# Attention and two feed-forwards on one core: gate and value by seven products of quarter blocks in place of eight

## The chip, the core and the metric

The kernel runs on one core of a Trainium2 chip. The metric is the device time of one execution in microseconds (us), from the first to the last instruction and a little around them. TensorE is called PE here and its loads of stationary operands PEld; VectorE is DVE, ScalarE is ACT, GpSimd is POOL, and SyncE, which issues the transfers, is SP.

## What is computed

Attention over 4 batches of 12 heads (448 tokens, 64 columns each), then a feed-forward with SiLU, then a second one with a gate and a value, all in float32. The part that the change touches is the last one, for 1792 tokens of 768 columns and 1536 hidden columns:

```python
def _moe2_ref(x, w_gate, w_val, w_out):
    g = x @ w_gate
    silu = g * (1.0 / (1.0 + np.exp(-g)))
    val = x @ w_val
    return (silu * val @ w_out).astype(np.float32)
```

## The kernel before

Each float32 matrix is held as two float16 parts, a high and a low one, and each product of matrices is three products of parts: high by high, high by low, low by high, summed in PSUM in float32. So each 128x128 piece of weights costs three matmuls, and each of them has a load of weights of its own.

The program is a list of operations with the engines that may run each, what each reads and writes, and a due time. A planner (`Plan.emit`) goes through the list once, when the program is built, keeps a clock for each engine by formulas for the length of each operation, and hands every operation to an engine and a place in its order; the numbers in `TUNE` (shifts of due times in `FINE`, `OFF`, `WIN`, `WOUT`; the letters A, D, P for the engines allowed; `CUT` for when the weights of the first feed-forward are loaded) steer it. The order on each engine is then fixed, and every queue, SP's too, runs in order: what waits holds up what stands behind it.

The stages overlap: attention of one batch (L706 scores, L816 probabilities by v) runs among the first feed-forward of the batch before it (`ffn1_h` L1011, `ffn1_o` L1051), which writes its result, transposed, to the DRAM tensor `x2d`. `load_gv` and `load_w_out2` bring the weights of the second feed-forward and split them; all of them then stay in SBUF.

The second feed-forward goes over the tokens in blocks of 512, 512, 512 and 256 columns. For a block, `bring_x2` loads x from `x2d` in six pieces of 128 rows, scales and splits them into `XT`. `ffn2_gv` goes over 12 chunks of 128 hidden columns: a chunk takes 6 pieces x 3 matmuls for the gate into one PSUM bank and as many for the value into another (L1206); ACT applies SiLU to the gate (L1211), DVE multiplies by the value out of PSUM (L1213), and ACT, DVE and POOL split the result into the high and the low part (L1216, L1217, L1218 or L1219) in `G`. Then `ffn2_out` takes 128 tokens at a time: two halves of 384 output columns, each 12 x 3 matmuls with the split activations as weights (L1250 to L1252), drained by ACT (L1255) and DVE (L1257) and stored to `out`. The output of one block and the gate and value of the next are interleaved on PE, and only four of the eight PSUM banks serve gate and value.

## Time and profile before

| | before |
|---|---|
| median of 3 runs | 1258.47 us (1258.27 to 1259.04) |
| the profiled execution, its own time | 1259.7 us |
| span of the profiled execution, first to last instruction | 1257.9 us |
| mean granted clock of TensorE over the span, of full speed | 0.98 |
| PE busy | 1178.2 us, 6612 matmuls |
| DVE, ACT, POOL busy | 687.2, 669.4, 492.0 us |
| moved by DMA | 140.61 MB |

The profile is one execution, taken by the hardware profiler. Busy time of an engine is the time in which at least one of its instructions ran; matmuls are pipelined, so several run at a time, and their mean length is longer than the step from one to the next. The granted clock is what TensorE's throttle let through, as a share of full speed. A releaser is whatever ended an idle stretch of an engine. L numbers are lines of the kernel before.

### The profile page before, as it was taken

What the parts mean: (1) busy time and instruction counts of PE and PEld (TensorE: products, weight loads), DVE (VectorE), ACT (ScalarE), POOL (GpSimd) and SP (SyncE); (2) the same over time, 40 slices, a digit from 0 to 9 for tenths busy, and PEclk for the clock granted to TensorE, in tenths of its full rate; (3) what the DMA queues carried; (4) which work ended last, traced back from release to release, by engine and by line L of the source; (5) the groups of instructions that cost most, each with busy time, mean ns of one, the idle gap of its engine ahead of it and who ended that gap; (6) DMA issues with size and microseconds to landing.
All of it is one profiled execution on the core that took longest, in us unless ns stands there. A gap on an engine that the chain in (4) does not pass through costs nothing.

```text
span 1257.9 us, 17505 instructions
## 1 busy us (share of the span) xinstructions
PE 1178.2 (94%) x6612; PEld 599.2 (48%) x6612; DVE 687.2 (55%) x1181; ACT 669.4 (53%) x1219; POOL 492.0 (39%) x474
## 2 busy tenths in 40 slices
PE   5989987799679999999999999999999999999998
PEld 3334443344334444444445454445544555446685
DVE  4788876688756575565459887873111301112121
ACT  4989967677669865898536435652111301112131
POOL 5565456454658897677721624120000100000000
PEclk9999999799889999999999999999999999999999
DMA  7565634479877688567774455502000101000101
GB/s 193 167 155 144 220 131 145 103 174 199 184 149 144 125 191 176 110 126 149 145 238 138 146 173 180 187 1 63 26 14 1 34 26 26 1 1 22 39 1 26
DMA packets 218581, 140.61 MB, mean 112 GB/s; under 512 B 156032, under 2 KB 210816, under 8 KB 218496
## 3 DMA queue, kind: packets, MB, share of 16 engines
q1 hardware_dynamic: 218496, 139.49, 44.3%
q8 instruction: 52, 0.85, 0.3%
q14 instruction: 33, 0.27, 0.1%
HBM read 85.79 MB, written 11.01 MB: 77 GB/s over the span
## 4 chain that ended last, share of the span: by engine, by line
PE 46%; DVE 5%; DMA 2%; POOL 1%; ACT 1%; issue 1%; POOLq 0%; ACTq 0%
PE ps L1206 25%; PE ps L1051 6%; PE ps L1250 4%; PE ps L1252 4%; PE ps L1251 4%; DMA ATT<-in_moe_w_val_dram 1%; DVE W L842 1%; PE ps L816 1%; PE ps L1011 1%; PE ps L706 1%; DVE ATT L890 1%; DVE G L1030 1%; DVE ATT L880 1%; DVE ATT L879 1%; DMA ATT<-ATT 1%
## 5 line engine op out<-in xcount | busy, mean ns | idle before, releaser
L1206 PE MATMUL ps<-XT,W 128*128 128x512 f16 (+1 forms) x1440 | 294.0, 352 | 3.8 <-ACT ER L1211 1.9
L1051 PE MATMUL ps<-G,W 128*128 128x448 f16 x1152 | 240.7, 355 | 4.0 <-DVE G L1041 4.0
L1011 PE MATMUL ps<-XT,W 128*128 128x448 f16 x1152 | 234.9, 353 | 8.2 <-ACT FT L1017 1.7
L1206 PEld LDWEIGHTS <-W 128*128 128x128 f16 x1440 | 141.0, 98 | 131.0 <-issue 5.1
L1011 PEld LDWEIGHTS <-W 128*128 128x128 f16 x1152 | 110.7, 99 | 120.5 <-issue 26.0
L1051 PEld LDWEIGHTS <-W 128*128 128x128 f16 x1152 | 107.9, 98 | 122.3 <-issue 28.9
L1216 ACT ACTIVATE G<-ER 128x512 f16<-128x512 f32 (+1 forms) x48 | 27.6, 575 | 167.3 <-DVE ER L1213 162.2
L1213 DVE SCALAR_TENSOR_TENSOR ER<-ER,ST,ps 128x512 f32<-128x512 f32 (+1 forms) x48 | 32.6, 680 | 151.5 <-PE ps L1206 151.4
L723 ACT ACTIVATE ER<-ps,ST 128x448 f32<-128x448 f32 x144 | 103.1, 719 | 12.1 <-POOL ATT L745 8.8
L1218 POOL TENSOR_SCALAR G<-ER 128x512 f16<-128x512 f32 x20 | 12.6, 629 | 245.5 <-DVE ER L1217 241.2
L715 DVE TENSOR_REDUCE ST<-ps 128x2 f32<-128x896 f32 x96 | 92.4, 966 | 27.8 <-PE ps L706 23.4
L1250 PE MATMUL ps<-W,G 128*128 128x384 f16 x308 | 100.4, 326 | 0.0
L1251 PE MATMUL ps<-W,G 128*128 128x384 f16 x308 | 100.4, 326 | 0.0
L1252 PE MATMUL ps<-W,G 128*128 128x384 f16 x308 | 100.4, 326 | 0.0
L1257 DVE SCALAR_TENSOR_TENSOR ATT<-ps,ST,ATT 128x384 f32<-128x384 f32 x28 | 17.3, 618 | 151.0 <-ACT ATT L1255 151.0
L1255 ACT ACTIVATE ATT<-ps,ST 128x384 f32<-128x384 f32 x28 | 16.2, 580 | 136.7 <-PE ps L1252 136.7
L745 POOL TENSOR_TENSOR ATT<-ER,ATT 128x448 f16<-128x448 f32 x77 | 86.0, 1117 | 6.4
L706 PE MATMUL ps<-ATT 128*64 128x448 f16 x560 | 75.3, 371 | 9.1 <-ACT ER L723 4.0
L1030 DVE SCALAR_TENSOR_TENSOR G<-FT,ST,G 128x448 f16<-128x448 f32 x64 | 57.5, 907 | 20.1 <-ACT G L1022 18.2
L744 POOL TENSOR_SCALAR ER<-ER,ST 128x448 f32<-128x448 f32 x77 | 56.7, 736 | 22.8 <-ACT ATT L739 11.8
L1206 PE MATMUL ps<-XT,ATT 128*128 128x512 f16 (+1 forms) x288 | 60.4, 352 | 0.0
L739 ACT ACTIVATE ATT<-ER,ST 128x448 f16<-128x448 f32 x71 | 45.5, 660 | 20.0 <-DVE ST L731 11.7
(221 smaller groups left out, 1889.4 us busy)
## 6 DMA issues: line engine op xcount, KB each, us to landing
ATT<-in_moe_w_out_dram SPq DMA_DIRECT2D x24, 768.0 KB, 4.3
W<-in_moe_w_in_dram SPq DMA_DIRECT2D x16, 768.0 KB, 6.1
ATT<-in_moe_w_gate_dram SPq DMA_DIRECT2D x12, 768.0 KB, 4.7
ATT<-in_moe_w_val_dram SPq DMA_DIRECT2D x12, 768.0 KB, 5.9
...
ATT<-in_v_dram SPq DMA_DIRECT2D x8, 672.0 KB, 7.2
...
```

The source lines that it names most:

```text
L706: nc.tensor.matmul(out=sp[64 * h:64 * h + 64, u, 0:S], lhsT=T[:, 0, t, 64 * h:64 * h + 64], rhs=T[:, a, :, 64 * h:64 * h + 64], start=(a = ...
L715: op(DVE, 1.04 * S * nt + 65, lambda sp=sp, nm=nm, nt=nt: nc.vector.tensor_reduce(nm, sp[:, 0:nt, 0:S], AX.X, ALU.max, negate=True), r=sk, ...
L723: op(ACT, 705, lambda e=e, u=u, t=t, sp=sp: nc.scalar.activation(e, sp[:, u, 0:S], AF.Exp, bias=st["nb"][:, t:t + 1], scale=eS, accum_out= ...
L744: nc.gpsimd.tensor_scalar(e, e, r1, 1.0, ALU.mult, ALU.mult)
L745: nc.gpsimd.tensor_tensor(lo, e, hi, ALU.subtract)
L1011: nc.tensor.matmul(out=ps[:, 0:S], lhsT=w[:, a, kk], rhs=xt1((b * HP + kk) % NX, x), start=(kk == 0 and s == 0), stop=(kk == KD - 1 and s ...
L1030: DVE: (t_stt(S), lambda gt=gt, hi=hi, lo=lo, s1=s1: nc.vector.scalar_tensor_tensor(lo, gt, s1, hi, ALU.mult, ALU.subtract), True),
L1051: nc.tensor.matmul(out=ps[:, 0:S], lhsT=w[:, a, P * m:P * m + P], rhs=GV1[:, f, x], start=(f == 0 and s == 0), stop=(f == NF1 - 1 and s == 2))
L1206: nc.tensor.matmul(out=ps[:, 0:n], lhsT=w[:, aa, kk], rhs=xt2(kk, x)[:, 0:n], start=(kk == 0 and s == 0), stop=(kk == KD - 1 and s == 2))
L1250: nc.tensor.matmul(out=ps[:, 0, 0:384], lhsT=hi, rhs=wh, start=(f == 0), stop=(f == NF2 - 1))
L1251: nc.tensor.matmul(out=ps[:, 1, 0:384], lhsT=hi, rhs=wlo, start=(f == 0), stop=False)
L1252: nc.tensor.matmul(out=ps[:, 1, 0:384], lhsT=lo, rhs=wh, start=False, stop=(f == NF2 - 1))
```

## The change

Gate and value of a block are a product of x (768 rows, in two halves of 384) with the two weight matrices. The block's tokens are cut into two halves, which makes the product one of a 2x2 arrangement of blocks by another; such a product takes eight products of blocks, and Winograd's form of Strassen's method takes seven, of sums and differences of the blocks.

- **Sums of weights.** `make_sums` makes, for each of the 12 chunks, four sums of quarter blocks of the gate's and the value's weights (ten operations of 384 columns on DVE), splits them (1536 columns: ACT the high part, DVE the low one) and stores them to a new DRAM tensor `s2d`. It is planned during block 0.
- **Sums of x.** `bring_sums` takes the place of `bring_x2` for blocks 1 to 3: three pieces; each loads two halves of x, makes four sums on DVE or POOL, and splits seven quarter blocks at once.
- **Seven products.** `ffn2_seven` takes the place of `ffn2_gv` for blocks 1 to 3: a chunk has seven products of 3 pieces x 3 matmuls, of half the block's columns; five PSUM banks a chunk, out of a ring of all eight; ACT copies the first product out, DVE adds the others to it in SBUF (five adds), and SiLU, the multiply and the split then read SBUF. The sums of weights come from `s2d` in two buffers, one load of 768 KB for each chunk.
- **Blocks** are of 512, 512, 384 and 384 tokens. Two of the four buffers `YS` now hold loaded sums, so the output has two in place of four.
- `FT` and `DG` become parts of one tile `FD`, whose 1024 columns serve as one of two buffers for the adds.
- The tables in `TUNE` are changed throughout: `FINE` (110 entries in place of 86), `OFF`, and many of the letters for engines; so the order of the earlier stages moves too.

```diff
-    PATIENCE={'silu': 2351.866, 'exp': 6600.368},
-    CUT=(0, 1, 1, 7, 10, 13, 16),
+    PATIENCE={'silu': 4305.451, 'exp': 12651.286},
...
+    CUT=(0, 1, 1, 11, 11, 13, 16),
...
-    WIN=83.7,
-    WOUT=99.3,
+    WIN=61.6,
+    WOUT=85.5,
...
+    SU='D',
+    SUH='A',
+    XU='DP',
...
-    FT = pool.tile([P, 2, S], F32, name="FT")
+    FD = pool.tile([P, 2 * S + 2 * P], F32, name="FD")
+    FT = FD[:, 0:2 * S].rearrange("p (a c) -> p a c", a=2)
+    DG = FD[:, 2 * S:].rearrange("p (a c) -> p a c", a=2)
...
+    s2d = dram.tile([NF2 * P, 3072], F16, name="s2d")
...
-    blocks = [(c, min(NB2, NT - c)) for c in range(0, NT, NB2)]
+    blocks = [(0, 512), (512, 512), (1024, 384), (1408, 384)]
+    assert sum(n for _, n in blocks) == NT
+    KH = KD // 2
...
+    T_GW = 82.0
...
+    XU = att32(O_XF, 1792)
+    XW = [XT[:, 3584 * i:3584 * i + 3584] for i in range(2)] + [ER.rearrange("p a c -> p (a c)").bitcast(F16)]
+
+    def bring_sums(i, z, due):
+
+        c0, n = blocks[i]
+        h = n // 2
+        bs = range(c0 // S, (c0 + n - 1) // S + 1)
+        s = s_x2[z][0]
+        if i == 1:
+            marker([], [("xf", r) for r in range(4)] + [("xu", 0, a) for a in range(2)] + [("ft2", r) for r in range(3)] + [(k, kk) for k in ("x2h", "x2l") for kk in range(KD)])
+        for kk in range(KH):
+            x = 0
+            xu, keys = XU[:, 0:7 * h], [("xf", r) for r in range(4)]
+            for a in range(2):
+                row = P * (kk + KH * a)
+                op(SP, t_dma(P * n * 4), lambda xu=xu, a=a, row=row: nc.sync.dma_start(out=xu[:, 5 * h * a:5 * h * a + n], in_=x2d[row:row + P, c0:c0 + n]),
+                   r=[("x2d", b, kk + KH * a) for b in bs] + ["attn_done"], w=[("xu", x, a)], due=due - 12 + kk, late=DMA_LATE)
+            t = xu.rearrange("p (s c) -> p s c", s=7)
+            ab = [("xu", x, 0), ("xu", x, 1)]
+            for d, a, b, alu in ((3, 6, 1, ALU.subtract), (1, 1, 0, ALU.subtract), (2, 3, 0, ALU.add), (4, 5, 2, ALU.subtract)):
+                add(only(TUNE["XU"], {
+                    DVE: (t_tt(h), lambda t=t, d=d, a=a, b=b, alu=alu: nc.vector.tensor_tensor(t[:, d], t[:, a], t[:, b], alu), True),
+                    POOL: (t_ptt(h), lambda t=t, d=d, a=a, b=b, alu=alu: nc.gpsimd.tensor_tensor(t[:, d], t[:, a], t[:, b], alu))}), r=ab, w=keys, due=due + kk)
+            split(XW[kk][:, 0:7 * h], XW[kk][:, 1792:1792 + 7 * h], xu, keys + ab, s, [("sx2", z), ("silu", B - 1)], [("x2h", kk)], [("x2l", kk)], due + kk, 7 * h)
+
+    US, SH = STG[0].bitcast(F32)[:, 0:1536], STG[1].bitcast(F16)[:, 0:3072]
+    SB = [(STG[2].bitcast(F16)[:, 0:3072], [("st2", 2)]), (ATT[:, (O_Y + 2 * CB) // 2:(O_Y + 4 * CB) // 2], [("ys", 2), ("ys", 3)])]
+
+    def make_sums():
+        marker([], ["U0", ("st2", 0)])
+        marker([], ["SHh", "SHl", ("st2", 1)])
+        us = US.rearrange("p (s c) -> p s c", s=4)
+        uk = [("U", s) for s in range(4)]
+        for f in range(NF2):
+            due = t_out2(0) + 6.0 * f
+            (gb, gk), (vb_, vk) = slot2(2 * f), slot2(2 * f + 1)
+            (gh, gl), (vh, vl) = [[t[:, 768 * a:768 * a + 768] for a in range(2)] for t in (gb, vb_)]
+            lo, hi = slice(0, 384), slice(384, 768)
+            for dst, terms in ((0, ((vh[:, lo], vh[:, hi], ALU.add), (vl[:, lo], ALU.add), (vl[:, hi], ALU.add))),
+                               (2, ((gh[:, lo], vh[:, lo], ALU.subtract), (gl[:, lo], ALU.add), (vl[:, lo], ALU.subtract))),
+                               (1, ((us[:, 0], gh[:, lo], ALU.subtract), (gl[:, lo], ALU.subtract))),
+                               (3, ((gh[:, hi], us[:, 1], ALU.subtract), (gl[:, hi], ALU.add)))):
+                for x, t in enumerate(terms):
+                    a, b, alu = t if x == 0 else (us[:, dst], *t)
+                    add(only(TUNE["SU"], {
+                        DVE: (t_tt(384), lambda dst=dst, a=a, b=b, alu=alu: nc.vector.tensor_tensor(us[:, dst], a, b, alu), True),
+                        POOL: (t_ptt(384), lambda dst=dst, a=a, b=b, alu=alu: nc.gpsimd.tensor_tensor(us[:, dst], a, b, alu))}),
+                        r=gk + vk + ["U0"] + [uk[0]] * (dst == 1) + [uk[1]] * (dst == 3), w=[uk[dst]], due=due)
+            sh, sl = SH[:, 0:1536], SH[:, 1536:3072]
+            add(only(TUNE["SUH"], {
+                ACT: (t_act(1536), lambda: nc.scalar.activation(sh, US, AF.Copy)),
+                DVE: (t_ts(1536), lambda: nc.vector.tensor_copy(sh, US), True),
+                POOL: (t_pts(1536), lambda: nc.gpsimd.tensor_scalar(sh, US, 1.0, 1.0, ALU.mult, ALU.mult))}), r=uk, w=["SHh"], due=due)
+            add(only(TUNE["SU"], {
+                DVE: (t_tt(1536), lambda: nc.vector.tensor_tensor(sl, US, sh, ALU.subtract), True),
+                POOL: (t_ptt(1536), lambda: nc.gpsimd.tensor_tensor(sl, US, sh, ALU.subtract))}), r=uk + ["SHh"], w=["SHl"], due=due)
+            op(SP, t_dma(P * 6144), lambda f=f: nc.sync.dma_start(out=s2d[P * f:P * f + P], in_=SH), r=["SHh", "SHl"], w=[("s2d", f)], due=due, late=DMA_LATE)
+
+    Z = [G[:, 12288:14336].bitcast(F32), FD[:, 0:1024]]
+    RING = [(PS_F[i], ("F", i)) for i in range(3)] + [(PS_X, "psx")] + [(PS_S[i][:, u], ("S", i, u)) for i in range(2) for u in range(2)]
...
+    def ffn2_seven(i, z):
+        c0, n = blocks[i]
+        h = n // 2
+        t0 = t_blk2(i)
+        step = 6.8 * n / 512.0
+        for f in range(NF2):
+            u = fn2[0]
+            fn2[0] += 1
+            sb, sbk = SB[u % 2]
+            op(SP, t_dma(P * 6144), lambda sb=sb, f=f: nc.sync.dma_start(out=sb, in_=s2d[P * f:P * f + P]), r=[("s2d", f)], w=sbk, due=t0 + step * (f - 2), late=DMA_LATE)
+            z4 = Z[u % 2]
+            zk = [("z", u % 2, x) for x in range(4)]
+            (g, gk), (v1, vk) = slot2(2 * f), slot2(2 * f + 1)
+            g, v1 = [t.rearrange("p (a k c) -> p a k c", a=2, k=KD) for t in (g, v1)]
+            sw = sb.rearrange("p (a s k c) -> p s a k c", a=2, s=4, k=KH)
+            at = [0]
+
+            def product(bank, o, w, wk, x):
+                ps, pk = bank
+                for kk in range(KH):
+                    def mm(kk=kk):
+                        for s, (aa, xx) in enumerate(((0, 0), (0, 1), (1, 0))):
+                            c = 1792 * xx + h * x
+                            nc.tensor.matmul(out=ps[:, h * o:h * o + h], lhsT=w[:, aa, kk], rhs=XW[kk][:, c:c + h],
+                                             start=(kk == 0 and s == 0), stop=(kk == KH - 1 and s == 2))
+                    op(PE, 3 * (h / 2.4 + 0.5), mm, r=wk + [("x2h", kk), ("x2l", kk)], w=[pk], due=t0 + step * f + 0.3 * at[0])
+                    at[0] += 1
+
+            def take():
+                bn2[0] += 1
+                return RING[bn2[0] % 8]
+
+            def plus(d, nd, bank, o, src, r):
+                ps, pk = bank
+                dst, pp, nn = z4[:, h * d:h * (d + nd)], ps[:, h * o:h * (o + nd)], nd * h
+                if src is None:
+                    sr = z4[:, 3 * h:4 * h].unsqueeze(1).to_broadcast([P, 2, h])
+                    dst, pp = dst.rearrange("p (a c) -> p a c", a=2), pp.rearrange("p (a c) -> p a c", a=2)
+                else:
+                    sr = z4[:, h * src:h * (src + nd)]
+                op(DVE, t_tt(nn), lambda: nc.vector.tensor_tensor(dst, pp, sr, ALU.add), r=[pk] + r, w=zk[d:d + nd], due=-1e4)
+            b1, b6, b2, b57, b34 = take(), take(), take(), take(), take()
+            product(b1, 0, g[:, :, 0:KH], gk, 0)
+            op(ACT, t_act(h, True), lambda z4=z4, ps=b1[0]: nc.scalar.activation(z4[:, 0:h], ps[:, 0:h], AF.Copy), r=[b1[1]], w=zk[0:1], due=-1e4)
+            product(b6, 0, sw[:, 1], sbk, 2)
+            plus(3, 1, b6, 0, 0, zk[0:1])
+            product(b2, 0, g[:, :, KH:KD], gk, 5)
+            plus(0, 1, b2, 0, 0, zk[0:1])
+            product(b57, 0, sw[:, 0], sbk, 1)
+            product(b57, 1, sw[:, 2], sbk, 3)
+            plus(1, 2, b57, 0, None, zk[3:4])
+            plus(3, 1, b57, 0, 2, zk[2:3])
+            product(b34, 0, sw[:, 3], sbk, 6)
+            product(b34, 1, v1[:, :, KH:KD], vk, 4)
+            plus(1, 2, b34, 0, 1, [])
+            gt, vt = z4[:, 0:n], z4[:, n:2 * n]
+            op(ACT, t_act(n, False, 1), lambda gt=gt, f=f: nc.scalar.activation(gt, gt, AF.Silu, scale=dg[:, f:f + 1]),
+               r=[("dg", f)], w=zk[0:2], due=-1e4, table="silu")
+            op(DVE, t_stt(n), lambda gt=gt, vt=vt, f=f: nc.vector.scalar_tensor_tensor(gt, gt, c2[:, f:f + 1], vt, ALU.mult, ALU.mult),
+               shared=True, r=[("c2", f)], w=zk, due=-1e4)
+            hi, lo = GV2[:, f, 0, 0:n], GV2[:, f, 1, 0:n]
+            op(ACT, t_act(n), lambda gt=gt, hi=hi: nc.scalar.activation(hi, gt, AF.Copy), r=zk[0:2], w=[("Gh", f)], due=-1e4)
+            op(DVE, t_tt(n), lambda gt=gt, hi=hi: nc.vector.tensor_tensor(gt, gt, hi, ALU.subtract), shared=True, r=[("Gh", f)], w=zk[0:2], due=-1e4)
+            add({POOL: (t_pts(n), lambda gt=gt, lo=lo: nc.gpsimd.tensor_scalar(lo, gt, 2.0 ** 11, 1.0, ALU.mult, ALU.mult)),
+                 ACT: (t_act(n), lambda gt=gt, lo=lo: nc.scalar.activation(lo, gt, AF.Copy, scale=2.0 ** 11))},
+                r=zk[0:2], w=[("Gl", f)], due=-1e4)
...
-    OT = YS
+    OT = YS[0:2]
...
-        ffn2_gv(i, zone(i))
+        (ffn2_seven if i else ffn2_gv)(i, zone(i))
+        if i == 0:
+            plan.tag = "sums"
+            make_sums()
+            plan.tag = None
         if i + 1 < len(blocks):
-            bring_x2(i + 1, zone(i + 1), t_blk2(i) + T_GV)
+            bring_sums(i + 1, zone(i + 1), t_out2(i))
```

The orders of DVE and SP around the place, as the program has them. First DVE, before, where the output of block 0 runs among the first chunks of block 1 (L1213 multiply, L1217 subtract, L1257 drain of the output):

```order
992 L1217 TENSOR_TENSOR ER<-ER,G 128x512
993 L1257 SCALAR_TENSOR_TENSOR ATT<-ps,ST,ATT 128x384 x6
994 L1213 SCALAR_TENSOR_TENSOR ER<-ER,ST,ps 128x512
995 L1217 TENSOR_TENSOR ER<-ER,G 128x512
996 L1257 SCALAR_TENSOR_TENSOR ATT<-ps,ST,ATT 128x384 x2
997 L1213 SCALAR_TENSOR_TENSOR ER<-ER,ST,ps 128x512
```

And DVE after the change at the same place (L1282 and L1291 make the sums of weights, L1340 are the adds of products, L1402 the drain of the output):

```order
1083 L1282 TENSOR_TENSOR ATT<-ATT,W 128x384 x6
1084 L1402 SCALAR_TENSOR_TENSOR ATT<-ps,ST,ATT 128x384
1085 L1282 TENSOR_TENSOR ATT<-W,ATT 128x384
1086 L1340 TENSOR_TENSOR G<-ps,G 128x256
1087 L1282 TENSOR_TENSOR ATT<-ATT,W 128x384
1088 L1340 TENSOR_TENSOR G<-ps,G 128x256
1089 L1402 SCALAR_TENSOR_TENSOR ATT<-ps,ST,ATT 128x384
1090 L1291 TENSOR_TENSOR ATT<-ATT 128x1536
1091 L1282 TENSOR_TENSOR ATT<-ATT 128x384
1092 L1340 TENSOR_TENSOR G<-ps,G 128x512
1093 L1282 TENSOR_TENSOR ATT<-ATT 128x384
1094 L1340 TENSOR_TENSOR G<-ps,G 128x256
```

The drains of products now stand in one queue with the sums of weights; row 1090 ends the eighth of twelve sums, and the last one ends at row 1190, among the adds of chunk 8 of block 1.

SP before, from the last weights on (L868 weights, L1186 x, L1261 output):

```order
265 L868 DMA ATT<-in_moe_w_out_dram 128x1536 x8
266 L1186 DMA ATT<-x2d 128x512 x6
267 L1261 DMA out_dram<-ATT 64x768 x8
268 L1186 DMA ATT<-x2d 128x512 x2
269 L1186 DMA ATT<-x2d 128x256 x4
```

And SP after, from the end of block 1's chunks to the start of block 3's x (L1293 stores sums of weights, L1309 loads them, L1252 x, L1406 output):

```order
293 L1293 DMA s2d<-ATT 128x3072
294 L1309 DMA ATT<-s2d 128x3072 x3
295 L1252 DMA ATT<-x2d 128x384 x4
296 L1406 DMA out_dram<-ATT 64x768 x2
297 L1252 DMA ATT<-x2d 128x384 x2
298 L1406 DMA out_dram<-ATT 64x768 x4
299 L1309 DMA ATT<-s2d 128x3072
300 L1406 DMA out_dram<-ATT 64x768 x2
301 L1309 DMA ATT<-s2d 128x3072 x11
302 L1252 DMA ATT<-x2d 128x384 x4
```

Where SP had nothing but x and outputs, each chunk now has a load of sums, which waits until PE is done with the buffer.

## Rows read from the trace of the kernel before

**Rows 1.** The page: busy time by engine, and the chain that ended last.

```profile
PE 1178.2 (94%) x6612; PEld 599.2 (48%) x6612; DVE 687.2 (55%) x1181; ACT 669.4 (53%) x1219; POOL 492.0 (39%) x474
...
PE 46%; DVE 5%; DMA 2%; POOL 1%; ACT 1%; issue 1%; POOLq 0%; ACTq 0%
PE ps L1206 25%; PE ps L1051 6%; PE ps L1250 4%; PE ps L1252 4%; PE ps L1251 4%; DMA ATT<-in_moe_w_val_dram 1%; DVE W L842 1%; PE ps L816 1%; PE ps L1011 1%; PE ps L706 1%; DVE ATT L890 1%; DVE G L1030 1%; DVE ATT L880 1%; DVE ATT L879 1%; DMA ATT<-ATT 1%
```

**Rows 2.** Windows: stretch and length, each engine's busy us, PE clock, DMA.

```profile
50.00:400.00 350.00, 301.99 (x1641) 142.66 (x1640) 268.12 (x488) 270.84 (x509) 196.39 (x173) 0.93 0.65 158
...
840.00:1200.00 360.00, 360.00 (x1965) 192.10 (x1964) 75.47 (x110) 71.27 (x116) 18.62 (x27) 1.00 0.08 22
```

**Rows 3.** Timeline of PE: start, length of the row, line, shape, number of matmuls.

```profile
842.07 10.52 PE L1206 MATMUL ps<-XT,W 128*128 128x512 f16 x48
...
1191.83 2.35 PE L1206 MATMUL ps<-XT,W 128*128 128x256 f16 x20
...
1249.69 0.33 PE L1251 MATMUL ps<-W,G 128*128 128x384 f16 x1
...
1252.29 0.33 PE L1252 MATMUL ps<-W,G 128*128 128x384 f16 x1
```

**Rows 4.** Groups of instructions, PEld: busy us, mean ns of one; idle before.

```profile
L1206 PEld LDWEIGHTS <-W 128*128 128x128 f16 x1440 | 141.0, 98 | 131.0 <-issue 5.1
```

**Rows 5.** Timeline of PEld: start, length of the row, number of loads.

```profile
122.53 0.11 PEld L1011 LDWEIGHTS <-W 128*128 128x128 f16 x2 [0.36 <-issue]
...
1191.94 2.06 PEld L1206 LDWEIGHTS <-W 128*128 128x128 f16 x19
```

**Rows 6.** Groups of instructions, DVE, by shape.

```profile
L1217 DVE TENSOR_TENSOR ER<-ER,G 128x512 f32<-128x512 f32 x36 | 27.7, 770 | 17.9 <-ACT G L1216 17.8
L1213 DVE SCALAR_TENSOR_TENSOR ER<-ER,ST,ps 128x512 f32<-128x512 f32 x36 | 26.9, 746 | 122.3 <-PE ps L1206 122.1
...
L1257 DVE SCALAR_TENSOR_TENSOR ATT<-ps,ST,ATT 128x384 f32<-128x384 f32 x28 | 17.3, 618 | 151.0 <-ACT ATT L1255 151.0
...
L842 DVE SCALAR_TENSOR_TENSOR XT<-ATT,ST,XT 128x512 f16<-128x512 f32 x12 | 9.0, 750 | 2.4 <-ACT XT L832 2.3
...
L1213 DVE SCALAR_TENSOR_TENSOR ER<-ER,ST,ps 128x256 f32<-128x256 f32 x12 | 5.8, 480 | 29.2 <-PE ps L1206 29.2
L1217 DVE TENSOR_TENSOR ER<-ER,G 128x256 f32<-128x256 f32 x12 | 5.1, 425 | 5.8 <-ACT G L1216 5.8
```

**Rows 7.** Groups of instructions, ACT and POOL, by shape.

```profile
L832 ACT ACTIVATE W<-W,ST 128x768 f16<-128x768 f32 x20 | 18.4, 935 | 1.0 <-DVE ST L457 1.0
...
L832 ACT ACTIVATE XT<-ATT,ST 128x512 f16<-128x512 f32 x14 | 10.0, 718 | 4.6 <-DMA ATT<-x2d 3.0 <-PE ps L1206 1.7
...
L595 POOL TENSOR_TENSOR SQ<-ATT,GX 128x256 f32<-128x256 f32 x16 | 13.9, 871 | 0.5
```

**Rows 8.** Windows of 20 us from 800 to 900 us, and their sum.

```profile
800.00:820.00 20.00, 20.00 (x95) 9.07 (x93) 16.59 (x25) 12.57 (x23) 1.91 (x1) 1.00 0.46 158
...
880.00:900.00 20.00, 20.00 (x118) 11.35 (x116) 1.92 (x4) 2.43 (x4) 0.00 (x0) 1.00 0.08 20
sum 100.00, PE 100.00 PEld 51.02 DVE 49.78 ACT 40.03 POOL 11.93; mean PE 20.00 PEld 10.20 DVE 9.96 ACT 8.01 POOL 2.39
```

**Rows 9.** Transfers: number, KB each, median us from issue to landing.

```profile
ATT<-in_moe_w_out_dram SPq DMA_DIRECT2D x24, 768.0 KB, 4.3
...
ATT<-in_v_dram SPq DMA_DIRECT2D x8, 672.0 KB, 7.2
...
ATT<-x2d SPq DMA_DIRECT2D x18, 256.0 KB, 3.0
```

65 lines of the change are left out of this document (34 added, 31 removed).

## Prediction

> **What bounds the kernel now.** I read the page first: PE is busy for 1178.2 us of a span of 1257.9 us, DVE, ACT and POOL for half of it or less, and the chain that ended last is PE for the largest part, with L1206 (the products of gate and value) as its biggest line [rows 1]. Then the windows, to see whether PE is busy everywhere [rows 2]: between 50 and 400 us it is idle for 48 us and runs at a mean granted clock of 0.93 of full speed, which is 2.4 GHz, so for some 14% of that stretch at 1.2 GHz; from 840 to 1200 us it is busy for 360.00 us of 360.00 at a clock of 1.00. That last stretch is the second feed-forward, which the change rewrites. There a transfer or another engine costs nothing so long as PE never waits, and a column fewer on PE is time gained. DVE, by contrast, is busy there for 75 us of 360 [rows 2]: this is the room for the work that the change adds.
>
> **Price of a product.** In the stretch at full clock I take the pitch of the matmuls, not their length, because they overlap: 48 of 512 columns in 10.52 us, the last one 0.38 long, are (10.52 - 0.38)/47 = 215.7 ns each; 20 of 256 columns are (2.35 - 0.27)/19 = 109.5 ns; of 384 columns 16 steps take 1252.29 - 1249.69 = 2.60 us, 162.5 ns each [rows 3]. The three lie on one line of 0.415 ns a column and 3.3 ns fixed. No row has 192 columns; the line gives 82.9 ns.
>
> **Removed and added on PE.** Before, a block has 12 chunks x 2 sides x 6 x 3 = 432 matmuls; three blocks of 512 columns and one of 256: 1296 x 215.7 + 432 x 109.5 = 279.5 + 47.3 = 326.8 us. After, block 0 stays (432 x 215.7 = 93.2), and each later block has 12 x 7 x 3 x 3 = 756 matmuls of half the block's columns: block 1 (512 tokens) 756 x 109.5 = 82.8, blocks 2 and 3 (384 each) 1512 x 82.9 = 125.3. Sum 301.3 us, so **25.5 us less**. The output products (14 tiles x 72 x 162.5 ns) are the same work in both, and so is the last drain behind them.
>
> **Weight loads.** Twelve products become seven of half the width, so there are more loads of weights per column. A load lasts 98 ns in the trace [rows 4], longer than the 82.9 ns. If loads could not overlap, 192 columns would cost at least 98 ns. In the 256 stretch 19 loads take 2.06 us, one per matmul, which decides nothing; but at 122.53 us two loads together take 0.11 us [rows 5], so the second began while the first ran, some 15 ns after it. I therefore take 82.9 ns, near this row, and keep 98 to 109 ns (the pitch of the 256 stretch) as the other end: 1512 x (98 - 82.9) = 23 us to 1512 x (109.5 - 82.9) = 40 us more. The Trainium skill, TensorE: Matmul & The Clock Gate, section LDWEIGHTS (loading the stationary operand), speaks against the change here: a load takes the number of weight columns over 1.2 GHz, which is an estimate of 107 ns for 128 columns. By that rule the sum would lose an estimated 36 us; the trace does not agree that 107 ns are spent one after the other, since its load lasts 98 ns and two fit in 0.11 us.
>
> **Added on DVE.** For each chunk of a seven-product block: three adds out of PSUM of half a block, two of a whole one, then the multiply and the subtraction as before. With 480 ns for 256 and 746 for 512 columns out of PSUM, and 770 for the subtraction [rows 6], a chunk of block 1 costs 3 x 480 + 2 x 746 + 746 + 770 = 4.4 us, while PE takes 63 x 109.5 = 6.9 us. For 192 and 384 columns, by 1.04 ns a column between those rows and by the 618 ns of 384: 3 x 413 + 2 x 618 + 618 + 637 = 3.7 us against 63 x 82.9 = 5.2 us. Neither waits for DVE alone. The **sums of weights** come on top, twelve times: ten operations of 384 columns (425 + 128 x 1.04 = 558 ns) and one of 1536 (425 + 1280 x 1.04 = 1.76 us), 7.3 us a chunk, 88 us in all, plus a copy on ACT of 1.6 us (0.93 us at 768 columns, 0.72 at 512 [rows 7]). Their cover is block 0 and its output: from 800 to 900 us DVE is busy for 50 us of 100 [rows 8]. DVE's order puts about eight of the twelve sums ahead of block 1's first add and the last four among the adds of its chunks 0 to 8. There DVE has 8 x 4.4 + 4 x 7.3 = 64 us to do while PE needs 55. The eight PSUM banks, five to a chunk, let PE run ahead by about one chunk (some 5 us). Bounds: 0, if DVE has caught up during block 0, and 12 us, if DVE arrives late from block 0 as well. I take **4 us lost**, nearer to the row sums than to 12 because of the slack.
>
> **Sums of x.** Three times per block: two loads (3.0 us [rows 9]), four sums and differences (0.43 us on DVE, 0.87 on POOL at 256 columns [rows 6, 7]), a split of 1792 columns (about 1.8 us on ACT, 2.1 on DVE by 1.04 ns a column from 0.75 at 512). That is 9 to 10.5 us, 26 to 31 us a block, behind the output stage of the block before: 8 x 36 x 162.5 ns = 46.8 us for 512 tokens, 35.1 us for 384, where it shrinks too. I cost it at nothing; without that cover it would be a stall of 4 us a block at most. At the edges of the blocks the ring of banks now includes those of the output stage; I take 1 us, bounds 0 and 4.
>
> **Loads of the sums.** Two buffers, 768 KB each per chunk, queued on SP behind a wait for PE. A buffer is free at the end of the sixth of seven products and needed at the second product two chunks later: 2 x 5.2 - 5 x 0.74 = 6.7 us. The nearest row, with the same 6 KB rows, is 4.3 us; the longest for a similar size is 7.2 [rows 9]. So it is hidden, and at 7.2 us each chunk would lose (7.2 - 6.7)/2 us, 6 us over 24 chunks. Behind these waiting issues on SP stand the output stores and the loads of the next x, which have a whole block's time.
>
> **The tables.** FINE, OFF, CUT and the engine choices move work in the first 700 us as well: from the feed-forward of the first batch on the orders of the engines differ at hundreds of places. No row prices such a reshuffle. What it can touch is the 48 us of idle PE and the half-clock time of 50 to 400 us [rows 2]. The trace gives no sign of direction, so 0, with a quarter of the idle time, 12 us, as the bound on both sides.
>
> **Sum.** -25.5 + 4 + 1 + 0 = -20.5 us. The profiled execution took 1259.7 us, 1.2 above the median of 1258.5; the difference applies to either: 1239 against it, **1238 us** as a median. Own range: 1226 to 1250.
>
> **Rivals.** (A) Loads of weights set the pitch at 192 columns: +23 to +40 us on 1238, so 1261 to 1278, slower than before. It decides from a pitch of 82.9 + 20.5/1.512 = 96.5 ns on. For it: loads of 98 ns; against it: two loads in 0.11 us. The page cited above would give about 1274 by its 107 ns. (B) DVE binds in block 1: sums made late because each waits for its copy, and for the store of the one before it (4.3 us or more), so that the adds behind them in DVE's queue leave PE without banks; the full 12 us instead of 4 and some at the edges: 1249. For it: 64 us of work for 55; against it: DVE half idle beforehand. (C) The moved tables open a new wait of 20 us or more in the first 700 us: 1259 or more. (D) They close more than 12 us of the old ones: about 1222. That the change does not do what it says is no rival: the order of the changed kernel shows 2268 matmuls of 256 and 192 columns.
>
> **Chances.** Forecast 0.70, B 0.12, A 0.10, C 0.04, D 0.04. A measurement of this kernel can tell about 0.2% (2.5 us) from no change. Faster by more: forecast, B and D, 0.86; slower: nearly all of A and C, 0.11; between, 0.03. The range of 8 in 10 takes in the forecast with the tables' bound and B, and leaves A and C out: 1221 to 1255.
>
> **What would show it.** In the profile after: PE busy throughout from block 0's end on; matmuls of 192 columns at 83 ns (rival A: 98 or more, PEld without gaps); idle time of PE in front of the new products put down to DVE in block 1 only, under 5 us; loads of the sums landing in about 4.3 us with no PE wait on them. The start of block 0 should be within 12 us of where it was; if it is not, the tables did it, and the forecast is off by that much.

## The result, and the profile after the change

| | before | after |
|---|---|---|
| median | 1258.76 us (1258.27 to 1259.12, 4 runs) | 1230.68 us (1228.05 to 1232.53, 4 runs) |
| ratio, with its 95% interval | | 0.9776 (0.9756 to 0.9796) |
| profiled execution, its span | 1259.7, 1257.9 us | 1232.5, 1230.7 us |

The change takes 28 us off. The forecast was 1238 us, with 1221 to 1255 as the range: the sign and the range held, and the forecast was some 7 us too slow. The changed kernel was timed twice more beside other kernels on other chips: 1228.1 us (ratio 0.9748, 0.9731 to 0.9765) and 1231.0 us (0.9754, 0.9735 to 0.9773).

The page of the changed kernel first, which answers to [rows 1]: busy time by engine, and the chain that ended last.

```profile
PE 1152.6 (94%) x7584; PEld 671.9 (55%) x7584; DVE 849.1 (69%) x1531; ACT 711.0 (58%) x1244; POOL 498.2 (40%) x473
...
PE 34%; DVE 11%; DMA 2%; POOL 2%; issue 1%; ACT 1%; POOLq 0%; ACTq 0%; DVEq 0%
```

PE is busy for 25.6 us less (1178.2 before); the sum of the prediction had 25.5. That it fits to 0.1 us is luck: the kernel before has 1175.6 us of busy PE in the run with the new tables below, with the same matmuls, and two more traces of the changed kernel have 1152.1 and 1150.6 us. DVE is busy for 162 us more and takes 11% of the chain in place of 5%, without becoming the bound. The span fell by 27.2 us, so PE's idle time changed by no more than 1.6 us as a whole. The windows, which answer to [rows 2], show that this small number is the difference of two larger ones.

```profile
50.00:400.00 350.00, 306.97 (x1679) 144.55 (x1676) 267.22 (x495) 274.42 (x510) 204.34 (x184) 0.94 0.66 159
400.00:708.00 308.00, 304.94 (x1801) 146.69 (x1801) 210.68 (x382) 210.91 (x370) 208.40 (x209) 1.00 0.70 160
...
840.00:1200.00 360.00, 354.03 (x3147) 285.88 (x3146) 226.13 (x407) 119.44 (x193) 26.10 (x29) 1.00 0.37 122
```

The row of before for 400 to 708 us, which did not stand ahead of the prediction:

```profile
400.00:708.00 308.00, 301.64 (x1780) 143.31 (x1779) 196.69 (x333) 216.03 (x405) 201.34 (x207) 1.00 0.67 153
```

From 50 to 400 us PE idles for 43.0 us in place of 48.0, from 400 to 708 us for 3.1 in place of 6.4: 8.3 us gained where the change rewrites no computation, only the tables. Block 0 starts at 699.4 us in place of 708.4. That is one trace of each, and the experiments show how far single traces can be trusted there. From 840 to 1200 us PE is no longer always busy: 6.0 us idle in place of none. What it waits for there is the view of the waits (PE from 840 us on; line, releaser, us in total, times, longest):

```profile
PE ps L1323 <- DMA ATT<-s2d: 3.0, 3, 2.4
PE ps L1395 <- DVE ATT L1402: 1.1, 2, 0.8
PE ps L1396 <- POOL W L1165: 0.9, 1, 0.9
PE ps L1396 <- ACT W L1163: 0.9, 1, 0.9
```

Half is the loads of sums of weights, half stands in the output of block 0 (the rows of L1395 and L1396 are its products): for the split of w_out and for drains on DVE. No row names an add of products on DVE (L1340), the wait that the prediction priced at 4 us.

The matmuls of the seven products, as a timeline of PE (start, length of the row, number):

```profile
1058.19 1.15 PE L1323 MATMUL ps<-XT,ATT 128*128 128x192 f16 x12
1059.18 0.66 PE L1323 MATMUL ps<-ER,ATT 128*128 128x192 f16 x6
```

Twelve matmuls of 192 columns from 1058.19 to 1059.18 us are 82.5 ns each, each with its own load of weights; the line through [rows 3] gave 82.9. DVE's new operations by shape (busy us, mean ns; idle before):

```profile
L1282 DVE TENSOR_TENSOR ATT<-ATT,W 128x384 f32<-128x384 f32 x70 | 40.7, 608 | 0.4
L1291 DVE TENSOR_TENSOR ATT<-ATT 128x1536 f16<-128x1536 f32 x12 | 21.3, 1772 | 2.0 <-ACT ATT L1287 2.0
...
L1340 DVE TENSOR_TENSOR FD<-ps,FD 128x512 f32<-128x512 f32 x12 | 8.3, 689 | 1.9 <-PE ps L1323 1.9
L1340 DVE TENSOR_TENSOR FD<-ps,FD 128x256 f32<-128x256 f32 x18 | 7.6, 422 | 0.9 <-ACT FD L1343 0.5
```

They came within some 60 ns of the estimates (558 ns and 1.76 us for the sums; 746 and 480 for the adds, which were taken from the multiply).

### The profile page after: what moved, and what is told of

Same layout as the page of the kernel before. It is cut to its first block, busy times and chain, and to the rows that moved or that the text cites. A ratio compares the mean times of both kernels' runs of the same rounds, so it can differ in the third digit from the quotient of the medians.

```text
span 1230.7 us, 19996 instructions
## 1 busy us (share of the span) xinstructions
PE 1152.6 (94%) x7584; PEld 671.9 (55%) x7584; DVE 849.1 (69%) x1531; ACT 711.0 (58%) x1244; POOL 498.2 (40%) x473
## 4 chain that ended last, share of the span: by engine, by line
PE 34%; DVE 11%; DMA 2%; POOL 2%; issue 1%; ACT 1%; POOLq 0%; ACTq 0%; DVEq 0%
PE ps L1323 16%; PE ps L1396 4%; PE ps L1397 4%; PE ps L1395 4%; PE ps L1056 4%; DVE ATT L1282 2%; DMA ATT<-s2d 2%; DVE ATT L885 1%; DVE ATT L1160 1%; PE ps L1016 1%; DVE W L847 1%; DVE ATT L895 1%; DVE ATT L884 1%; DVE G L1035 1%; DVE ATT L1291 1%
## 5 line engine op out<-in xcount | busy, mean ns | idle before, releaser
L1016 PEld LDWEIGHTS <-W 128*128 128x128 f16 x1152 | 110.4, 99 | 119.0 <-issue 25.2
L1056 PEld LDWEIGHTS <-W 128*128 128x128 f16 x1152 | 107.5, 98 | 117.6 <-issue 23.3
L1323 PEld LDWEIGHTS <-ATT 128*128 128x128 f16 x1458 | 131.0, 99 | 12.2 <-DMA ATT<-s2d 3.8
L1323 PE MATMUL ps<-XT,ATT 128*128 128x192 f16 (+1 forms) x972 | 121.3, 257 | 3.0 <-DMA ATT<-s2d 3.0
L1396 PE MATMUL ps<-W,G 128*128 128x384 f16 x308 | 100.4, 326 | 1.8 <-POOL W L1165 0.9
L1395 PE MATMUL ps<-W,G 128*128 128x384 f16 x308 | 100.4, 326 | 0.0
L1220 PE MATMUL ps<-XT,W 128*128 128x512 f16 x360 | 85.8, 379 | 3.9 <-ACT ER L1225 1.6
L1323 PEld LDWEIGHTS <-W 128*128 128x128 f16 x810 | 73.3, 98 | 6.0
L1402 DVE SCALAR_TENSOR_TENSOR ATT<-ps,ST,ATT 128x384 f32<-128x384 f32 x28 | 17.3, 617 | 84.1 <-ACT ATT L1400 84.1
L1323 PE MATMUL ps<-XT,W 128*128 128x192 f16 (+1 forms) x540 | 73.5, 255 | 0.0
L1323 PE MATMUL ps<-ER,ATT 128*128 128x192 f16 (+1 forms) x486 | 66.2, 256 | 0.0
L1035 DVE SCALAR_TENSOR_TENSOR G<-FD,ST,G 128x448 f16<-128x448 f32 x64 | 51.4, 815 | 20.5 <-ACT G L1027 18.8
L839 POOL TENSOR_SCALAR XT<-ATT,ST 128x1344 f16<-128x1344 f32 (+1 forms) x4 | 5.5, 1380 | 143.4 <-PE ps L1323 143.0
```

What stands on the lines that cost most here:

```text
L1016: nc.tensor.matmul(out=ps[:, 0:S], lhsT=w[:, a, kk], rhs=xt1((b * HP + kk) % NX, x), start=(kk == 0 and s == 0), stop=(kk == KD - 1 and s ...
L1035: DVE: (t_stt(S), lambda gt=gt, hi=hi, lo=lo, s1=s1: nc.vector.scalar_tensor_tensor(lo, gt, s1, hi, ALU.mult, ALU.subtract), True),
L1056: nc.tensor.matmul(out=ps[:, 0:S], lhsT=w[:, a, P * m:P * m + P], rhs=GV1[:, f, x], start=(f == 0 and s == 0), stop=(f == NF1 - 1 and s == 2))
L1220: nc.tensor.matmul(out=ps[:, 0:n], lhsT=w[:, aa, kk], rhs=xt2(kk, x)[:, 0:n], start=(kk == 0 and s == 0), stop=(kk == KD - 1 and s == 2))
L1323: nc.tensor.matmul(out=ps[:, h * o:h * o + h], lhsT=w[:, aa, kk], rhs=XW[kk][:, c:c + h], start=(kk == 0 and s == 0), stop=(kk == KH - 1 a ...
L1395: nc.tensor.matmul(out=ps[:, 0, 0:384], lhsT=hi, rhs=wh, start=(f == 0), stop=(f == NF2 - 1))
```

## Experiments

The theory after the first trace: the seven products brought what was forecast, and the 7 us on top come from the tables, in the first 700 us. Rivals: the tables do nothing by themselves; DVE or the loads cost more or less than priced. Ratios are to the kernel before, run beside each kernel; the medians of before were 1260.0, 1259.7 and 1261.7 us in the three sets of runs.

### The tables alone

The kernel before, with nothing changed but `TUNE`, which is that of the changed kernel.

> The kernel before (eight products, blocks 512, 512, 512, 256), with the whole table TUNE of the changed kernel. Theory: the part of the gain that I did not forecast comes from the tables, since after the change block 0's products start at 699.4 us in place of 708.4 and PE is idle for 8.3 us less up to 708 us. Then this kernel takes 1249 us (9 less than before, 1247 to 1252), with block 0 starting near 699 us. Rival: the tables are worth nothing by themselves with eight products, and the earlier start only shifts work of the first feed-forward behind it: 1258 us, within 3.

Measured: 1251.35 us, ratio 0.9938 (0.9915 to 0.9960), so 8.6 us less (by the interval 5 to 11). Its windows:

```profile
50.00:400.00 350.00, 308.13 (x1686) 145.77 (x1683) 268.27 (x497) 275.31 (x511) 206.19 (x185) 0.95 0.66 160
400.00:708.00 308.00, 303.76 (x1796) 146.02 (x1795) 208.38 (x380) 209.35 (x368) 207.73 (x208) 1.00 0.71 160
```

The idle time before 708 us is that of the changed kernel (41.9 and 4.2 us), with eight products behind it, and block 0 starts at 699.2 us, as expected. Set side by side by their number in PE's order, the 4500th matmul (in the output of block 0) and the last one both start 9.4 us earlier than in the kernel before, so all of it stands ahead of them. This is the part of the gain that the prediction did not have.

### The seven products alone

The changed kernel with `TUNE` of before.

> The changed kernel with the table TUNE of the kernel before (sums of weights on DVE and of x on DVE or POOL, as in the change). Theory: seven products alone are worth 18 to 20 us, so 1240 us (1237 to 1244), with block 0 starting near 708 us. Rival: the tables do nothing by themselves, 1231 us; second rival: the old tables fit the new second half badly (DVE's order of sums and drains), 1250 us or more.

Measured: 1248.8 us (1244.5 to 1253.1), ratio 0.9917 (0.9889 to 0.9944): 11 us less than before (7 to 14 by the interval), a little over half of what was expected, between the theory and its second rival. If tables and products only added, 8.6 and 11 us would make 20, and the change brings 28.

Block 0 was expected near 708 us and starts at 702.6. Up to 685 us this kernel and the kernel before run the same instructions in the same order on every engine, so the order can't be what makes these 6 us; scatter between executions is the likely cause, which a second trace of the kernel before would have to show. With the new tables block 0 starts between 696.0 and 699.7 us in all eleven traces. So the tables do move it forward, but what that is worth is better read from the medians (8.6 us, 5 to 11) than from 708.4 against 699.4.

The longest waits of PE from 840 us on in this kernel (its profiled execution, with 1244.5 us the fastest of the five):

```profile
PE ps L1323 <- DMA ATT<-s2d: 4.5, 2, 4.0
PE ps L1395 <- DVE ATT L1402: 2.6, 1, 2.6
PE ps L1323 <- DVE FD L1340: 1.5, 1, 1.5
...
```

The longest stands at 980 us. The chain of waits shows what led to it, row by row in order of time (start, us, what):

```profile
969.16 1.48 ACT ATT L1287
970.66 1.77 DVE ATT L1291
972.45 3.22 DMA s2d<-ATT
975.74 4.29 DMA ATT<-s2d
980.08 6.26 PE ps L1323 x36
```

This is the eleventh of the twelve sums of weights: high part on ACT, low part on DVE, store, load, and only then PE, in chunk 10 of block 1. In DVE's order its low part stands among the adds of chunk 9 with these tables, and behind those of chunk 6 in the changed kernel. Late sums are what rival B named, but the path is another: B had PE wait for banks that late adds hold, and here it waits above all for the load of the sum (4.5 us), for adds on DVE (L1340) 3.4 us in all. The next two kernels take the tables apart.

### The tables in two parts

First the early tables of before (`FINE`, `CUT`, `WIN`, `WOUT`, letters and offsets up to the first feed-forward) in the changed kernel; then the other way round.

```diff
-    OFF={... 'gv': 130.5, 'x2': 154.8, ... 'o3': 73.8, 'w2': -99.0, ... 'f2': -82.9, ... 'sums': 16.8},
+    OFF={... 'gv': 130.5, 'x2': 181.6, 'o3': 150.3, 'w2': -104.8, 'f2': -90.5},
```

(The diff is the core of the second one; GVY, GVH, GVL, O2S, O2H, O2L and PATIENCE go with it.)

> The changed kernel with the tables of the kernel before for the earlier stages (FINE, CUT, WIN, WOUT, T_ATT and all letters and offsets up to the first feed-forward), and the changed tables for the second one. In DVE's order the last sum of weights stands among the adds of chunk 8 of block 1, as in the changed kernel. Theory: the tables have two separate effects, and this loses only the first, the idle time of PE before 700 us: 1237 us (1234 to 1240), with PE idle in block 1 under 1 us. Rival: old and new tables don't mix and what is lost is all of it, 1245 us or more.

> The changed kernel with its own tables for the earlier stages and those of the kernel before for the second feed-forward (offsets of gate and value, x, w_out and its split, their letters, PATIENCE; no offset of the sums). In DVE's order the last sum of weights now stands among the adds of chunk 10 of block 1 in place of chunk 8. Theory: the stages before 700 us are as in the changed kernel, and the second effect of the tables is lost: the store and the load of the last sums come too late for chunk 11, PE waits 5 to 9 us in block 1, 1236 us (1233 to 1241). Rival: the place of the last sum doesn't matter, 1229 us within 2.

Measured: with the early tables of before 1242.7 us, ratio 0.9848 (0.9830 to 0.9866); with the late ones 1233.7 us, 0.9775 (0.9755 to 0.9795). Beside the changed kernel in the same set (1231.0 us) that is 11.7 and 2.7 us lost. The second is not clear of the scatter: the changed kernel's ratio in this set is 0.9754 (0.9735 to 0.9773). The first is more than the theory had. Its waits:

```profile
PE ps L1396 <- ACT W L1163: 3.8, 2, 2.7
PE ps L1396 <- POOL W L1165: 2.7, 2, 1.6
...
```

Block 0 starts 2.8 us later there (702.4 us against 699.7 in the changed kernel's trace of this set), and the first product of its output 5.8 us later (848.4 against 842.6): this is the effect that the theory named, in its size. But the output of block 0 also waits 6.5 us for the split of w_out (1.8 us in the changed kernel), and behind these waits PE's clock fell, as the windows show:

```profile
860.00:870.00 10.00, 4.54 (x20) 2.02 (x18) 9.38 (x9) 5.65 (x5) 7.17 (x6) 0.70 0.19 79
870.00:880.00 10.00, 9.57 (x50) 5.41 (x49) 8.35 (x10) 4.16 (x4) 3.06 (x4) 0.78 0.52 172
```

A hundred matmuls into that output the lag is 12.1 us, and 12.3 at the end. So half of the loss is a second effect of the early tables, which neither theory nor rival had.

With the late tables of before the expected wait came, if dearer in the trace than in the time: PE waits for loads of sums

```profile
PE ps L1323 <- DMA ATT<-s2d: 7.4, 4, 4.6
```

where the changed kernel of the same set waits 0.5 us. Its profiled span, 1232.6 us, is 6.4 us over that one's 1226.2, but the medians differ by 2.7 only; how much of the 7.4 us is in every execution stays open. The longest wait stands behind the store of the twelfth sum, which took 7.6 us in this trace where the one in the chain above took 3.2. The net of this trace hides two larger numbers: the 5000th matmul, in block 1, starts 5.5 us ahead of the changed kernel's (934.2 against 939.7), and the 6000th, behind the late sums, 6.4 us after it (1061.7 against 1055.3). The kernel with all tables of before loses 18 to 21 us against the changed one, and the two parts added make 14.4; its interval of 7 us leaves open whether that difference is real.

### Do loads of weights bind at narrow matmuls?

The last two blocks of the changed kernel as 512 and 256 tokens, so that the products of the last block have 128 columns.

```diff
-    blocks = [(0, 512), (512, 512), (1024, 384), (1408, 384)]
+    blocks = [(0, 512), (512, 512), (1024, 512), (1536, 256)]
```

> The changed kernel with blocks of 512, 512, 512 and 256 tokens in place of 512, 512, 384, 384, so the last block's products have 128 columns. By columns alone the PE work is the same (756 x 109.5 + 756 x 56.4 = 125.4 us against 1512 x 82.5 = 124.7 us). Theory: a load of weights of 98 ns hides behind matmuls of 192 columns but takes over below some width; if it binds at its own length at 128 columns, the pitch is 98 ns and the kernel takes 1231 + 756 x 0.0416 = 1262 us. Rival: two loads run one in the other, the pitch follows the columns at 56 to 60 ns, and the time is 1231 us, within 4. A pitch between the two, at 64 ns or so, would give 1237.

Measured: 1230.2 us (1226.8 to 1231.4), ratio 0.9771 (0.9746 to 0.9796): no difference to the changed kernel, whose three ratios in other sets are 0.9748 to 0.9776. The timeline of PE, and below it that of the loads of weights, in the last block:

```profile
1169.28 0.83 PE L1323 MATMUL ps<-XT,ATT 128*128 128x128 f16 x12
...
1171.29 0.83 PE L1323 MATMUL ps<-XT,W 128*128 128x128 f16 x12
...
1169.23 2.05 PEld L1323 LDWEIGHTS <-ATT 128*128 128x128 f16 x36
...
L1323 PEld LDWEIGHTS <-ATT 128*128 128x128 f16 x1458 | 124.0, 98 | 15.5 <-DMA ATT<-s2d 1.9
```

From 1169.28 to 1171.29 us there are 36 matmuls (the row shown and three more), 55.8 ns each, and 36 loads of weights in 2.05 us, though one load still lasts 98 ns. Loads run one in the other, and even at 128 columns the columns set the pace. Rival A is dead by a wide margin, and the hint against it, two loads in 0.11 us [rows 5], was the row to trust. The Trainium skill, TensorE: Matmul & The Clock Gate, section Back-to-back issue gap, gives 81 ns for a stream of pairs of a load and a matmul of 128 columns and 131 ns for 512; here the rows show 55.8 and 215.7, so the measurement decides. The section's other formula, N / 2.4 + 2.5 ns, which it keeps for a single matmul, agrees within half a nanosecond with all four widths here: 55.8 and 82.5, and from [rows 3] 109.5 and 215.7.

### What the sums of weights cost on DVE

Three kernels: the sums made for one chunk only; all sums, but later; and the sums shared with POOL.

```diff
-        for f in range(NF2):
+        for f in range(1):
...
-            op(SP, ... in_=s2d[P * f:P * f + P]), r=[("s2d", f)], w=sbk, ...
+            op(SP, ... in_=s2d[0:P]), r=[("s2d", 0)], w=sbk, ...
```

> The changed kernel with the sums of weights made and stored for the first chunk alone; all twelve chunks of blocks 1 to 3 load that one set, so eleven twelfths of the sums are left out and 80 us of DVE with them, while every load, product and add stays. Theory: DVE costs little because block 0 covers it; what remains is PE's 3.0 us of waits at 854 to 862 us (splits of w_out2 and drains of the output that stand behind sums in DVE's queue) and 0.5 us at 911 us; so 1227.5 us, 3 to 4 less than the changed kernel. Rival: those waits have another cause (the splits of w_out2 are late by their own chain), and the sums cost nothing: 1231 us. Second rival: the sums cost 4 us or more in block 1 as predicted: 1224 us or less.

Measured: 1225.1 us (1223.4 to 1225.6), ratio 0.9724, beside 1228.1 us for the changed kernel: 3.0 us, in the theory's size and place, though the intervals touch (0.9706 to 0.9742 here, 0.9731 to 0.9765 there). PE from 840 to 1200 us waits for nothing but

```profile
PE ps L1323 <- DMA ATT<-s2d: 0.3, 1, 0.3
PE ps L1323 <- ACT G L1343: 0.2, 1, 0.2
```

so the waits in the output of block 0 for the split of w_out and for drains were the sums' doing. In the changed kernel the splits on DVE stand between the sums, in one queue. (The planner uses the room: 11 more sums of x go to DVE in place of POOL, so DVE is busy for 62 us less, not for the 80 that were expected. The waits for the split are gone in the next kernel too, which keeps all sums and starts them behind it; it gains 3.6 us on the changed kernel in the output of block 0.)

```diff
-                        r=gk + vk + ["U0"] + [uk[0]] * (dst == 1) + [uk[1]] * (dst == 3), ...
+                        r=gk + vk + ["U0", "w2_done"] + [uk[0]] * (dst == 1) + [uk[1]] * (dst == 3), ...
```

> The changed kernel with one dependency more: no sum of weights before all of w_out2 is split, which moves the first sum from 799 us to about 835 us and takes away part of the cover that block 0 gives. Theory: DVE has 179 us of work in the 200 us from 780 to 980 us, so some 20 us of slack; sums that start 36 us later cannot end in time, the adds and the last loads of sums wait, and the kernel takes 1248 us (1240 to 1256), with PE waiting on DVE or on loads of sums in block 1. Rival: there is more slack than that, since PE can run ahead and block 1 needs sum f only at chunk f: 1233 us or less.

Measured: 1248.2 us (1244.6 to 1249.5), ratio 0.9913 (0.9892 to 0.9934), as expected. PE waits 10.4 us for loads of sums, in six places. The chain shows the same piece as with the old tables again and again; this is the tenth sum (start, us, what):

```profile
957.49 1.49 ACT ATT L1287
959.01 1.76 DVE ATT L1291
960.79 3.57 DMA s2d<-ATT
964.43 4.21 DMA ATT<-s2d
968.69 5.78 PE ps L1323 x36
```

From the copy behind the last addition of a sum to the product that needs it are 11.2 us (957.49 to 968.69), and 7.9 of them are the way to memory and back. The sums started at 837 us in place of 798; of these 39 us, 20 show in the time.

```diff
-    SU='D',
+    SU='DP',
```

> The changed kernel with the sums of weights on DVE or POOL, as the planner picks (SU='DP'), in place of DVE alone; POOL is busy for 23 of the 200 us from 780 to 980 us. Theory: less DVE work by some tens of us, the waits at 854 to 862 us shrink, 1229 us (2 less). Rival: POOL takes over twice as long for one operation (871 ns at 256 columns against 425 on DVE), a sum is a chain of such operations, and so sums come late for the first chunks of block 1: 1236 us or more.

Measured: 1262.6 us (1260.7 to 1267.6), ratio 1.0027 (1.0013 to 1.0042): 34 us more than the changed kernel, the rival's way and far beyond its price. PE waits 19.5 us for loads of sums. The groups of POOL from 780 to 1060 us, then those of DVE from 800 to 860 us:

```profile
L1283 POOL TENSOR_TENSOR ATT<-ATT,W 128x384 f32<-128x384 f32 x64 | 70.2, 1117 | 1.7 <-DVE ATT L1282 0.7
L1292 POOL TENSOR_TENSOR ATT<-ATT 128x1536 f16<-128x1536 f32 x12 | 37.8, 3150 | 20.9 <-ACT ATT L1287 20.8
...
L1160 DVE SCALAR_TENSOR_TENSOR ATT<-W,ST 128x768 f32<-128x768 f32 x11 | 17.5, 1588 | 5.7 <-ACT W L1156 4.7 <-POOL W L1158 0.8
L1231 DVE TENSOR_TENSOR ER<-ER,G 128x512 f32<-128x512 f32 x7 | 9.6, 1375 | 0.8 <-ACT G L1230 0.8
L1227 DVE SCALAR_TENSOR_TENSOR ER<-ER,ST,ps 128x512 f32<-128x512 f32 x7 | 5.2, 742 | 2.8 <-PE ps L1220 2.7
```

The same three groups of DVE in the changed kernel, 800 to 860 us:

```profile
L1160 DVE SCALAR_TENSOR_TENSOR ATT<-W,ST 128x768 f32<-128x768 f32 x11 | 11.5, 1044 | 0.7 <-POOL W L1158 0.7
L1227 DVE SCALAR_TENSOR_TENSOR ER<-ER,ST,ps 128x512 f32<-128x512 f32 x7 | 5.2, 741 | 0.0
L1231 DVE TENSOR_TENSOR ER<-ER,G 128x512 f32<-128x512 f32 x7 | 4.8, 682 | 0.0
```

All twelve low parts (L1292) and 104 of the 120 additions went to POOL, at twice DVE's time or near it, one after the other. And DVE's own operations on two operands in SBUF grew from 1044 to 1588 and from 682 to 1375 ns, while the one that reads PSUM stayed at 742. Part of the work taken off DVE came back as longer operations: the three groups take 32.3 us in place of 21.5. How much of the 34 us is due to POOL's own pace and how much to DVE's slower operations was not separated.

### What the loads of the sums cost

In blocks 2 and 3 four buffers for loaded sums in place of two (the two in which the sums were made are free by then), and loads planned four chunks ahead.

```diff
+    ... SB4 = SB + [(SH, ["SHh", "SHl"]), (STG[0].bitcast(F16)[:, 0:3072], [("U", s) for s in range(4)])]
...
-            sb, sbk = SB[u % 2]
-            op(SP, ... due=t0 + step * (f - 2), late=DMA_LATE)
+            sb, sbk = SB[u % 2] if u < NF2 else SB4[u % 4]
+            op(SP, ... due=t0 + step * (f - (2 if u < NF2 else 4)), late=DMA_LATE)
```

> The changed kernel with four buffers in place of two for the loaded sums of weights in blocks 2 and 3 (the two more lie in the buffers that made the sums, free by then), and their loads planned four chunks ahead. Theory: the waits of PE on these loads at 1036 and 1139 us (2.4 and 0.2 us idle), and the half clock that follows the first (some 30 matmuls of 192 columns at 160 ns in place of 82.5, 2.3 us), go away: 1226 us, 4 to 5 less than the changed kernel, and no matmul of 192 columns above 85 ns. Rival: the loads are late because SP issues them late behind output stores, and four buffers leave that as it is: 1231 us.

Measured: 1227.75 us (1226.5 to 1228.0), ratio 0.9747 (0.9726 to 0.9768). This set held no changed kernel, so a later one put both side by side:

> The changed kernel as it is, beside the other kernels of this call. All theories: 1228 to 1233 us, by 20 to 30 us less than the kernel before, with the same idle places of PE (three waits of 0.8 to 1 us between 854 and 861 us, one of 2 to 3 us when block 2's third load of sums is late).

> The changed kernel as it is, beside the other kernels of this call: 1226 to 1233 us in every theory. The wait for a load of sums near 1032 to 1036 us was 2.4 us in one trace and 0.5 us in another, so the single times should scatter by some 3 us.

> Four buffers for the loaded sums in blocks 2 and 3 once more, this time beside the changed kernel itself. Theory: it is faster than the changed kernel by the wait for the loads of sums and the half clock behind it, 1 to 4 us depending on how late the load comes in a run, and its times scatter less. Rival: the same within 1 us, since the waits are rare.

Measured in the set with both: 1227.0 us (1226.6 to 1227.9) with four buffers, ratio 0.9727 (0.9711 to 0.9744), and 1231.0 us (1228.0 to 1232.0) for the changed kernel. So 4.0 us by the medians, and a smaller scatter. But the changed kernel's interval there, 0.9735 to 0.9773, overlaps, and in another set it took 1228.1 us (0.9748), which is the ratio of four buffers in their first set: the gain is not clear of noise. In the first trace of the changed kernel, an execution of 1232.5 us, PE waits 2.37 us at 1036 us for a load that was issued at 1029.45 and took 6.2 us. In its other two traces, of 1226.7 and 1228.0 us, the load took 4.4 us and the wait is 0.5 us; the two traced executions with four buffers took 1226.5 and 1226.6. That fits a long wait in some executions of the changed kernel only; the untraced ones can't be told apart by it. The timeline of PE and the windows around it, first trace:

```profile
1032.71 0.66 PE L1323 MATMUL ps<-ER,W 128*128 128x192 f16 x6
1035.74 2.07 PE L1323 MATMUL ps<-XT,ATT 128*128 128x192 f16 x18 [2.37 <-DMA ATT<-s2d]
...
1035.00:1040.00 5.00, 4.26 (x33) 4.11 (x34) 1.45 (x3) 1.14 (x2) 0.00 (x0) 0.68 0.02 6
1042.00:1050.00 8.00, 8.00 (x100) 8.00 (x98) 5.69 (x13) 4.01 (x9) 0.00 (x0) 1.00 0.56 191
```

Behind the wait the clock is 0.68 for 5 us: 33 matmuls take 4.26 us, 100 take 8.00 a little later, so some 1.6 us went to the clock on top of the 2.4. The second trace of the changed kernel at the same place, the matmuls behind the wait and the window:

```profile
1031.69 1.66 PE L1323 MATMUL ps<-XT,ATT 128*128 128x192 f16 x18 [0.49 <-DMA ATT<-s2d]
...
1028.00:1034.00 6.00, 5.51 (x64) 5.15 (x63) 3.33 (x8) 1.18 (x3) 0.00 (x0) 1.00 0.66 197
```

With four buffers the same stretch has no wait and a clock of 1.00:

```profile
1028.00:1034.00 6.00, 6.00 (x70) 5.61 (x69) 2.40 (x6) 0.91 (x2) 0.00 (x0) 1.00 0.62 198
1034.00:1040.00 6.00, 6.00 (x75) 6.00 (x74) 4.43 (x11) 2.96 (x6) 0.00 (x0) 1.00 0.39 135
```

Of the kernels that compute the whole result it has the lowest medians, by less than the scatter between sets.

## Why the prediction was right, and where it was off

**PE's work: right.** 25.5 us were forecast, PE's busy time fell by 25.6, and by 23.0 to 25.0 from the kernel with the new tables and eight products (1175.6 us) to the three traces of the changed one. What shows the mechanism is the pitch: 82.5 ns for 192 columns where the line gave 82.9.

**Loads of weights: right**, and with more room than the bound had: no cost at 192 columns, none at 128.

**DVE: the size right by luck, the place wrong.** 4 us were forecast in block 1; leaving out the sums gave back 3.0, and they stood in the output of block 0, where the split of w_out shares DVE's queue with the sums. That queue had not been gone through in the prediction: the neighbours named were the adds and drains behind it. In block 1 the prediction had 64 us of DVE work for 55 us of PE; DVE was busy for 52 us of the 55 from 905 to 960 us, and no add made PE wait. The last sum ends at 962 us, behind the adds of chunk 8, and chunk 11 is the first to need it.

**Rival B: late sums are real, but not here, and their cost takes another path.** With late sums the kernels lose 18 to 21 us (all old tables, which do more than delay the sums), 20 us (a start after the split of w_out) and 34 us (POOL). PE waits there above all for the loads of sums (4.5, 10.4 and 19.5 us), which the prediction costed at nothing, and less for the adds that B named (3.4, 4.6 and 3.3 us). Two to three chunks' delay of a sum is enough for such a wait; the kernel with the late tables of before alone has the delay too and loses only 2.7 us on balance, since its trace was ahead until then.

**Edges of the blocks and sums of x: right enough.** 1 us was forecast, with 0 as the lower bound; no wait of PE on them is in the list after.

**Loads of the sums: wrong at one place.** They were costed at nothing, by a slack of 6.7 us in a steady run of chunks. The loads are late where the run is not steady: the first two chunks of block 2 are spread among the output of block 1, so when chunk 0 gives its buffer free at 1029.45 us, chunk 1 is nearly done too, and chunk 2 needs its load 3.9 us later (1029.45 to 1033.37), less than the usual 4.3. That cost 0.5 us of waiting in two traces, and 2.4 us in the one where the load took 6.2; the gain by four buffers lies between nothing and 4.0 us, within the bound of 6.

**The tables: the term that was mis-sized.** Set at 0 with 12 us on both sides; measured as 8.6 us with eight products (5 to 11). It is why the forecast was 7 us too slow: with -8.6 in place of 0 the sum gives 1229 us, and the errors of the other terms about cancel. Rival D named this direction, with more than 12 us.

With seven products the early tables are worth 11.7 us, but in the trace only half of that stands ahead of block 0's output; the other half is waits for the split of w_out and the clock behind them, and no term of the sum had that. So it is no proof of the sum that this kernel's ratio of 0.9848 makes 1239.3 us of the median of 1258.5, against the 1238 forecast. The kernel with all the tables of before is as plain a reading of "tables at 0", and it takes 1248.8 us. That the old tables throw away more than half of the gain was not foreseen: the prediction read the place of the sums from the changed order and did not say that this place is itself a product of the tables. Which entries of the early tables close the idle time was not tried and stays open.

**The signs.** Of those listed, the pitch of 192 columns and block 0's start within 12 us came true. PE is not busy throughout from block 0's end on, its idle time is not put down to DVE in block 1, and it does wait for loads of sums. The range held, with the largest error, the tables, on the fast side.
